# Low parts of the weights on VectorE instead of GpSimd, and a shorter general path

## The chip, the cores and the metric

One Trainium2 chip, one of its cores. The metric is the time on the device for one execution of the program, in microseconds. The kernel before took 546.93 us (median of 3 runs, 546.54 to 547.39).

## What is computed

The reference is a gated linear recurrence over 768 steps for 4 x 8 heads of 48 channels, followed by a feed-forward block over the 3072 tokens that come out of it:

```python
for t in range(S):                                   # B, H, S, D = 4, 8, 768, 48
    state = alpha[:, :, t, :, None] * state + k_t (x) v_t
    y[:, :, t] = q_t @ state
x = y as (B*S, H*D)                                  # 3072 x 384
h = x @ w_in                                         # w_in 384 x 2048
g = h * tanh(softplus(h))
out = g @ w_out                                      # w_out 2048 x 384
```

`q`, `k`, `v` and `alpha` are float32; the weights come as float64, which on the chip are pairs of 32-bit words.

## The kernel before

**Two paths.** `fast_path` computes the result and, beside it, a set of conditions on the inputs (no overflow, no vanishing decay, weights in range). They end in one word, `good` (L886). All five engines load that word (L1018) and branch on it (L1019): if a condition fails, `general_path` computes everything again in a slow and safe way; if all hold, they jump over its code to the end of the program. With the inputs timed here they jump. The general path's instructions stand in each engine's stream between the branch and the place where it lands.

**The fast path.** The 768 steps are cut into 24 chunks of 128 steps (4 batches, 6 chunks each). For each chunk `attention(n)` loads q, k and alpha (`qka`, two buffers) and v, makes running products of alpha with two scans on VectorE (L472, L484), scales k and q (L480, L494), forms the scores on TensorE (L508), masks them (L516), forms y (L531) and updates the state (L499, L658). y is split into a high and a low part in fp32r, the inputs of the feed-forward block.

The feed-forward block runs in 106 units, `unit(c0, nt, f, ...)`: `nt` chunks (2 or 4) times one of 16 slices `f` of the hidden channels. A unit is 9 matmuls up (L695), a chain of ScalarE and VectorE work on the result (L703 to L729) and 3 matmuls down for each chunk (L764). Every factor is held as a high and a low part, so each product takes three matmuls.

**The weights.** `weight(f)` prepares slice f of both weight matrices (m = 0, 1), 32 preparations in all. VectorE builds the float32 word from the two halves of the float64 (L352, L357, L362), ScalarE rounds it to the high part `hi` (L367), and GpSimd subtracts `hi` from the word to give the low part `lo` (L370). `lo` is needed by the matmuls of the units of slice f.

**The order.** All of it is written as tasks with an engine, a cost (time on the engine, time until the result is there), a due key and dependencies. `Plan.order` runs through them as a list scheduler and emits each engine's instructions in the order that it finds: of the tasks that can begin soonest it takes the one with the lowest key. Tasks marked `port=True` share one resource in the plan (VectorE and GpSimd work on SBUF never overlap in it). Where the plan finds TensorE idle for longer than a filler matmul and 0.1 us, between its times 2.4 and 130 us, it emits a filler (L822), a matmul on zeros whose result is overwritten. The plan only sets the order; on the chip every instruction waits for its semaphores.

**The fillers before.** The first 16 are bf16 with 384 columns; the 63 after them take nine forms in groups of seven (bf16 or fp32r, 96 or 128 rows and columns, 128 to 512 columns wide); the rest are again bf16 with 384 columns.

Of the kernel before, what the change touches and what calls it, by code (L numbers as in the profile page):

```python
# [9 lines left out]
F32 = mybir.dt.float32  # L10
F32R = mybir.dt.float32r
BF16 = mybir.dt.bfloat16
I32 = mybir.dt.int32
U32 = mybir.dt.uint32
AF = mybir.ActivationFunctionType
# [13 lines left out]
P = 128  # L29
# [28 lines left out]
CHECK_FROM = 45.0  # L58
CHECK_STEP = 2.0
COLD = 16  # L60
EACH = 7
FORMS = [
    (False, P, P, DM, True), (True, P, P, DM, True), (True, P, 96, DM, True),
    (True, P, P, 512, True), (True, P, P, 256, True), (False, P, 96, DM, True),
    (True, P, P, DM, False), (True, 96, P, DM, True), (True, P, P, 128, True),
]
LAST_FORM = COLD + EACH * len(FORMS)
FILL_BANKS = ("o3", "o2", "o1", "o0", "h")
FILL_FROM, FILL_UNTIL = 2.4, 130.0
FILL_MARGIN = 0.1  # L70
EARLY_BANKS = {}
X_PE = 8
W_PE = 0
W_PE_BANKS = ["o2"]
MOVER = lambda n, s, r: "SP"

# [19 lines left out]
class Plan:  # L96
# [121 lines left out]
COST = {  # L218
    "load part": (0.7, 3.3), "load q": (1.8, 5.0), "load v": (0.7, 4.0), "load w": (2.0, 5.0),
    "move": (0.63, 2.5), "store": (0.47, 3.0),  # L220
    "cold fill": (0.321, 0.36), "off": (0.4, 0.65), "w off": (0.95, 1.2), "lead": (0.27, 0.38), "bits": (0.47, 0.58), "w hi": (0.42, 0.56), "w lo": (0.95, 1.08),
    "w check": (0.92, 1.2),
    "scan": (1.16, 1.27), "inverse": (0.09, 0.21), "mult": (0.6, 0.72), "check": (0.2, 0.34),
    "state": (0.365, 0.4), "state0": (0.31, 0.35), "mask": (0.63, 0.77),
    "scores": (1.1, 1.35), "y0": (1.1, 1.4), "y": (2.0, 2.25), "turn": (0.4, 0.65),
    "turned": (0.43, 0.57), "update": (0.75, 1.05),
    "x3 hi": (0.16, 0.3), "x3 lo": (0.2, 0.32), "x hi": (0.39, 0.53), "x lo": (0.48, 0.59),
    "down": (0.531, 0.8), "stash": (0.4, 0.53), "join": (0.47, 0.59), "result": (0.5, 0.7),
}
for _n in range(1, 5):  # L230
    _c = 128 * _n
    COST["up", _n] = (9 * (0.4333e-3 * _c + 0.009), 9 * (0.4333e-3 * _c + 0.009) + 0.25)
    COST["exp", _n] = (0.22 + 0.836e-3 * _c, 0.32 + 0.836e-3 * _c)
    COST["act", _n] = (0.105 + 0.836e-3 * _c, 0.24 + 0.836e-3 * _c)
    COST["ln", _n] = (0.19 + 0.836e-3 * _c, 0.33 + 0.836e-3 * _c)
    COST["dve", _n] = (0.075 + 1.045e-3 * _c, 0.19 + 1.045e-3 * _c)

for _n in (128, 256, DM, 512):
    for _real in (False, True):
        _c = _n / 2400 + (0.017 if _real else 0.0035)  # L240
        COST["fill", _real, _n] = (_c, _c + 0.03)

EXPLORE = None

# [1 line left out]
def fast_path(ctx, tc, qka, v, w, out, good):  # L246
# [84 lines left out]
    def weight(f):  # L331
# [12 lines left out]
        for m in range(2):  # L344
            hi, lo = (wo[:, z, f : f + 1, :] if m else wi[:, z, :, fs] for z in range(2))
            as_hi = lambda t, hi=hi: t.rearrange("p (s f) -> p s f", f=hi.shape[-1])
            lead = plan.buffer("lead")
            words = lambda z, m=m: stage.tile[:, m, :, z]

            def begin(m=m, lead=lead, words=words):  # L350
                new(lead, [P, DM], f"w_lead{f}_{m}", dtype=I32)
                nc.vector.tensor_scalar(  # L352
                    lead.tile, words(1), 3, 0x3FFFFFF8, ALU.logical_shift_left, ALU.bitwise_and
                )

            def signs(lead=lead, words=words):
                nc.vector.scalar_tensor_tensor(  # L357
                    lead.tile, words(1), -0x40000000, lead.tile, ALU.bitwise_and, ALU.bitwise_or
                )

            def ends(lead=lead, words=words):
                nc.vector.scalar_tensor_tensor(  # L362
                    lead.tile, words(0), 29, lead.tile, ALU.logical_shift_right, ALU.bitwise_or
                )

            def upper(lead=lead, hi=hi, as_hi=as_hi):
                nc.scalar.activation(hi, as_hi(lead.tile.bitcast(F32)), AF.Copy)  # L367

            def lower(lead=lead, hi=hi, lo=lo, as_hi=as_hi):
                nc.gpsimd.tensor_tensor(  # L370
                    lo, as_hi(lead.tile.bitcast(F32)), hi.bitcast(F32), ALU.subtract
                )

            k = key + 0.5 * m
            t = add("DVE", *COST["lead"], k, begin, [got], [stage, lead], port=True)
            t = add("DVE", *COST["bits"], k + 0.01, signs, [t], [stage, lead], port=True)
            t = add("DVE", *COST["bits"], k + 0.02, ends, [t], [stage, lead], port=True)
            a = add("ACT", *COST["w hi"], k + 0.03, upper, [t], [lead])
            if f < W_PE:
                bank = plan.buffer(W_PE_BANKS[(2 * f + m) % len(W_PE_BANKS)])  # L380

                def off(bank=bank, lead=lead, hi=hi, as_hi=as_hi, m=m):
                    p = new(bank, [P, NPAIR * C], f"w{f}_{m}", ps)[:, :DM]
                    nc.tensor.matmul(p, ident, lead.tile.bitcast(F32), start=True, stop=False)
                    nc.tensor.matmul(as_hi(p), minus_ident, hi, start=False, stop=True)

                def left(bank=bank, lo=lo, as_hi=as_hi):
                    nc.scalar.activation(lo, as_hi(bank.tile[:, :DM]), AF.Copy)

                t = add("PE", *COST["w off"], k + 0.04, off, [a], [lead, bank])  # L390
                b = add("ACT", *COST["w hi"], k + 0.05, left, [t], [bank])
            else:
                b = add("POOL", *COST["w lo"], k + 0.04, lower, [a], [lead], port=True)
            ready_w[f, m] = [a, b]
# [412 lines left out]
            add("SP", *COST["store"], k, store, [written], [osb])  # L807

    nothing = const.tile([P, NPAIR * C], BF16, name="nothing")  # L810
    nc.vector.memset(nothing, 0.0)
    none_r = const.tile([P, NPAIR * C], F32R, name="none_r")
    nc.scalar.activation(none_r, nothing, AF.Copy)

    def fill(buffer, i):
        real, rows, cols, n, start = FORMS[max(i - COLD, 0) // EACH] if i < LAST_FORM else FORMS[0]
        of = none_r if real else nothing

        def fill():
            if buffer.tile is None:  # L820
                buffer.make()
            nc.tensor.matmul(  # L822
                buffer.tile[:cols, :n], of[:rows, :cols], of[:rows, :n], start=start, stop=True,
                skip_group_check=True,
            )

        return Task("PE", *COST["cold fill" if i < COLD else ("fill", real, n)], None, fill, False)

    plan.fill = fill

# [58 lines left out]
def general_path(ctx, tc, q, k, v, alpha, w_in, w_out, out):  # L889

    nc = tc.nc
    T = 16
    BH = B * H
    dram = ctx.enter_context(tc.tile_pool(name="dram", bufs=1, space=bass.MemoryType.DRAM))
    x_d = dram.tile([B * S, DM], F32, name="x_d")
# [23 lines left out]
                nc.sync.dma_start(dst[:, ds(t0, T), :], yt[b * H : (b + 1) * H])  # L919

    with tc.tile_pool(name="conv", bufs=1) as sb:
        W = 512
        for m, src in enumerate((w_in, w_out)):
            words = src.rearrange("r c -> (r c)").bitcast(I32).rearrange("(p c) -> p c", p=P)
            with tc.For_i(0, DM * FF // P, W) as c0:
                t = sb.tile([P, W, 2], I32, tag="t", name=f"t{m}")
                nc.sync.dma_start(t.rearrange("p c w -> p (c w)"), words[:, ds(c0 * 2, 2 * W)])
                low, high = t[:, :, 0].bitcast(U32), t[:, :, 1]
                lead = sb.tile([P, W], I32, tag="lead", name=f"lead{m}")
                unit = sb.tile([P, W], I32, tag="unit", name=f"unit{m}")  # L930
                f = sb.tile([P, W], F32, tag="f", name=f"f{m}")
                z = sb.tile([P, W], F32, tag="z", name=f"z{m}")
                nc.vector.tensor_scalar(
                    lead, high, 3, 0x3FFFFFF8, ALU.logical_shift_left, ALU.bitwise_and
                )
                nc.vector.scalar_tensor_tensor(
                    lead, high, -0x40000000, lead, ALU.bitwise_and, ALU.bitwise_or
                )
                nc.vector.tensor_scalar(unit, lead, -0x800000, None, ALU.bitwise_and)
                nc.scalar.activation(f, low, AF.Copy, scale=2.0**-52)  # L940
                nc.vector.tensor_tensor(f, f, unit.bitcast(F32), ALU.mult)
                nc.vector.tensor_tensor(f, f, lead.bitcast(F32), ALU.add)
                nc.scalar.activation(z, high.bitcast(F32), AF.Square)
                nc.vector.tensor_scalar(lead.bitcast(F32), z, W_SMALL, -1.0, ALU.is_lt, ALU.mult)
                nc.vector.scalar_tensor_tensor(
                    f, lead.bitcast(F32), 1.0, f, ALU.add, ALU.mult
                )
                nc.vector.tensor_scalar(z, z, W_LARGE, -1.0, ALU.is_lt, ALU.mult)
                nc.vector.tensor_scalar(z, z, 1.0, 3e38, ALU.add, ALU.mult)
                nc.vector.scalar_tensor_tensor(f, z, 1.0, f, ALU.add, ALU.mult)  # L950
                nc.sync.dma_start(w_d[m][:, ds(c0, W)], f)

    with tc.tile_pool(name="moe", bufs=1) as sb, tc.tile_pool(name="pm", bufs=1, space=PSUM) as ps:
        ident = sb.tile([P, P], F32, name="ident_g")
# [131 lines left out]
```

## Time and profile before

| | us |
|---|---|
| median of 3 runs | 546.93 |
| the profiled execution, its own time | 546.43 |
| its span, from the first to the last instruction | 544.7 |
| TensorE busy | 532.1 (98%) |
| VectorE busy | 400.9 (74%) |
| ScalarE busy | 396.5 (73%) |
| GpSimd busy | 51.6 (9%) |
| DMA, mean rate | 100 GB/s |

PE is TensorE, PEld its weight load, DVE is VectorE, ACT ScalarE, POOL GpSimd, SP the queue that issues the DMAs. A "q" behind an engine's name is its sequencer: instructions that wait, load registers or branch. Busy shares are means over stages with different limits. Fillers count as busy time of TensorE. Instructions of one engine overlap a little: the next starts before the end of the last is recorded.

### The profile page before, as it was taken

How to read it: one execution, taken by the hardware profiler on the slowest of the kernel's cores; microseconds unless marked ns; L12 is line 12 of the kernel's file. 1: busy time of each engine (PE TensorE's matmuls, PEld its weight loads, DVE VectorE, ACT ScalarE, POOL GpSimd, SP SyncE). 2: the span in 40 equal slices, each digit the busy share in tenths (PEclk: the TensorE clock that was granted, in tenths of full speed). 3: DMA queues.
4: the chain of work that ended last, by engine and by line, in shares of the span. 5: the costliest groups of instructions: out<-in, count | busy, mean ns of one | idle time of the engine just before them, and what ended most of it. 6: DMA issues, size and time to landing. Idle time of an engine off the chain costs nothing.

```text
span 544.7 us, 9438 instructions
## 1 busy us (share of the span) xinstructions
PE 532.1 (98%) x3405; PEld 471.8 (87%) x3405; DVE 400.9 (74%) x715; ACT 396.5 (73%) x907; POOL 51.6 (9%) x45
## 2 busy tenths in 40 slices
PE   7999999999999999999999999999999999999994
PEld 4787899988898888888899888899988889998994
DVE  7999999999998699777974567885458744545441
ACT  1565779999688997997867755567775567787773
POOL 2222104514331000000000000000000000000000
PEclk9999999999999999999999999999999999999998
DMA  7665536221453677556220032220042000010001
GB/s 246 191 171 177 163 86 205 63 112 58 143 157 117 193 235 259 176 190 192 71 72 2 29 102 74 74 73 1 5 126 75 9 7 1 14 45 1 1 0 63
DMA packets 21812, 54.20 MB, mean 100 GB/s; under 512 B 4000, under 2 KB 14752, under 8 KB 21760
## 3 DMA queue, kind: packets, MB, share of 16 engines
q1 hardware_dynamic: 21760, 53.55, 32.1%
q8 instruction: 28, 0.46, 0.4%
q14 instruction: 24, 0.20, 0.1%
HBM read 46.45 MB, written 4.72 MB: 94 GB/s over the span
## 4 chain that ended last, share of the span: by engine, by line
PE 81%; DVE 11%; DMA 4%; ACT 1%; issue 1%; SPq 0%; ACTq 0%
PE o L764 35%; PE h L695 33%; PE y L531 6%; PE sc L508 4%; DMA qka<-in_qka_dram 4%; PE u L646 2%; DVE rest L472 2%; PE kb L637 1%; DVE probs L516 1%; DVE qka L484 1%; DVE w_lead L357 1%; DVE w_lead L352 1%; DVE y L713 1%; DVE w_lead L362 1%; DVE t L722 1%
## 5 line engine op out<-in xcount | busy, mean ns | idle before, releaser
L764 PE MATMUL o<-wo,g 128*128 128x384 f32 x1152 | 229.2, 342 | 0.0
L695 PE MATMUL h<-xs,wi 128*128 128x512 f32 (+1 forms) x954 | 218.3, 373 | 0.4 <-DVE y L713 0.4
L764 PEld LDWEIGHTS o<-wo,g 128*128 128x128 f32 x1152 | 202.0, 188 | 9.5 <-issue 0.7
L695 PEld LDWEIGHTS h<-xs,wi 128*128 128x128 f32 x954 | 167.5, 188 | 27.1 <-DVE y L713 0.7
L703 ACT ACTIVATE u<-h 128x512 f32<-128x512 f32 (+1 forms) x106 | 58.8, 554 | 90.7 <-PE h L695 90.5
L713 DVE SCALAR_TENSOR_TENSOR y<-u,h 128x512 f32<-128x512 f32 (+1 forms) x106 | 67.0, 633 | 54.0 <-ACT u L703 53.5
L729 DVE TENSOR_TENSOR g<-t,g 128x512 fp32r<-128x512 f32 (+1 forms) x106 | 68.7, 649 | 50.6 <-ACT g L726 50.3
L716 ACT ACTIVATE t<-t,tenth 128x512 f32<-128x512 f32 (+1 forms) x106 | 71.9, 679 | 2.1
L722 DVE SCALAR_TENSOR_TENSOR t<-y,t 128x512 f32<-128x512 f32 (+1 forms) x106 | 67.4, 636 | 8.1 <-ACT t L719 7.8
L726 ACT ACTIVATE g<-t 128x512 fp32r<-128x512 f32 (+1 forms) x106 | 61.6, 582 | 8.6 <-DVE t L722 6.2
L709 ACT ACTIVATE t<-u 128x512 f32<-128x512 f32 (+1 forms) x106 | 62.7, 591 | 3.2 <-DVE g L729 0.7
L719 ACT ACTIVATE t<-t 128x512 f32<-128x512 f32 (+1 forms) x106 | 61.6, 581 | 0.7
L472 DVE TENSOR_TENSOR_SCAN rest<-qka,behind 112x516 f32<-112x516 f32 x24 | 31.6, 1317 | 8.7 <-DMA qka<-in_qka_dram 8.7
L516 DVE COPY_PREDICATED probs<-causal,sc 128x512 f32<-128x512 uint32 x48 | 32.6, 728 | 1.9 <-PE sc L508 1.8
L508 PEld LDWEIGHTS sc<-qka 48*128 48x128 f32 x384 | 24.1, 187 | 8.2 <-issue 4.2
L484 DVE TENSOR_TENSOR_SCAN qka<-qka,ahead 112x516 f32<-112x516 f32 x24 | 31.0, 1293 | 0.0
L370 POOL TENSOR_TENSOR wo<-w_lead,wo 128x384 fp32r<-128x384 f32 x16 | 26.0, 1623 | 50.7 <-ACT wo L367 50.7
L508 PE MATMUL sc<-qka 48*128 48x128 f32 x384 | 28.8, 285 | 1.7 <-ACT wo L367 1.1
L370 POOL TENSOR_TENSOR wi<-w_lead,wi 128x384 fp32r<-128x384 f32 x16 | 22.2, 1390 | 66.0 <-ACT wi L367 66.0
L531 PE MATMUL y<-probs,v 128*64 128x128 f32 (+1 forms) x384 | 26.6, 278 | 0.3 <-DVE ahead L477 0.2
L531 PEld LDWEIGHTS y<-probs,v 128*64 128x64 f32 (+1 forms) x384 | 20.5, 129 | 4.3 <-DVE probs L516 1.1
L531 PE MATMUL y<-qka,state 112*112 112x128 f32 x160 | 20.9, 273 | 0.0
(78 smaller groups left out, 408.1 us busy)
## 6 DMA issues: line engine op xcount, KB each, us to landing
qka<-in_qka_dram SPq DMA_DIRECT2D x23, 674.2 KB, 5.3
ws<-in_wp_dram SPq DMA_DIRECT2D x16, 768.0 KB, 4.8
wc<-in_wp_dram SPq DMA_DIRECT2D x16, 768.0 KB, 4.9
v<-in_vp_dram SPq DMA_DIRECT2D x24, 192.0 KB, 3.4
out_dram<-osb SPq DMA_DIRECT2D x16, 192.0 KB, 1.9
xs<-x SPq DMA_DIRECT2D x144, 16.0 KB, 2.4
out_dram<-part SPq DMA_DIRECT2D x8, 192.0 KB, 2.4
qka<-in_qka_dram SPq DMA_DIRECT2D x2, 224.0 KB, 3.7
```

The source lines that it names most:

```text
L508: nc.tensor.matmul(p[a][:, j], K()[r : r + D, j], Q()[r : r + D, j], start=True, stop=True)
L531: nc.tensor.matmul(o, l, r, start=m < (2 if first else 1), stop=m >= len(ops) - 2, skip_group_check=True,)
L695: nc.tensor.matmul(p[:, :N], wi[:, z, s, fs], x[:, a, s], start=m == 0, stop=m == len(passes) - 1)
L703: nc.scalar.activation(wide(u), wide(h), AF.Exp, scale=-1.0, accum_out=uchk[:, at : at + 1])
L709: nc.scalar.activation(wide(t), wide(u), AF.Square, bias=1.0, scale=2.0)
L713: nc.vector.scalar_tensor_tensor(wide(y), wide(u), 0.5, wide(h), ALU.add, ALU.mult)
L716: nc.scalar.activation(wide(t), wide(t), AF.Ln, bias=tenth, scale=0.1)
L719: nc.scalar.activation(wide(t), wide(t), AF.Exp, scale=-1.0)
L722: nc.vector.scalar_tensor_tensor(wide(t), wide(y), 0.4, wide(t), ALU.mult, ALU.mult)
L726: nc.scalar.activation(g.tile[:, 0, :N], wide(t), AF.Copy)
L729: late[mybir.EngineType.DVE] = nc.vector.tensor_tensor(g.tile[:, 1, :N], wide(t), g.tile[:, 0, :N].bitcast(F32), ALU.subtract)
L764: made = nc.tensor.matmul(o.tile[:, :DM], g.tile[:, a, j * C : (j + 1) * C], wo[:, z, f], start=begins and m == 0, stop=end and m == 2,)
```

## The change

The low part of every weight slice is computed by VectorE (`f >= W_DVE` holds for all f, with `W_DVE = 0`), with the cost 0.47 us in the plan instead of 0.95 us. The fillers all take one form. `none_r` and the ScalarE instruction that writes it go; `nothing` becomes 384 columns wide. Some costs of the plan are set anew. The general path takes two steps to a turn of its recurrence loop instead of 16, and converts both weight matrices in one loop with tiles half as wide instead of two loops.

```diff
-EACH = 7
-FORMS = [
-    (False, P, P, DM, True), (True, P, P, DM, True), (True, P, 96, DM, True),
...
-LAST_FORM = COLD + EACH * len(FORMS)
...
+W_DVE = 0
...
-    "cold fill": (0.321, 0.36), "off": (0.4, 0.65), "w off": (0.95, 1.2), "lead": (0.27, 0.38), "bits": (0.47, 0.58), "w hi": (0.42, 0.56), "w lo": (0.95, 1.08),
+    "cold fill": (0.321, 0.36), "fill": (0.1635, 0.2), "off": (0.4, 0.58), "w off": (0.95, 1.2), "lead": (0.27, 0.38), "bits": (0.47, 0.58), "w hi": (0.42, 0.56), "w lo": (0.95, 1.08),
...
-    "scores": (1.1, 1.35), "y0": (1.1, 1.4), "y": (2.0, 2.25), "turn": (0.4, 0.65),
-    "turned": (0.43, 0.57), "update": (0.75, 1.05),
+    "scores": (1.12, 1.28), "y0": (1.1, 1.16), "y": (2.0, 2.02), "turn": (0.4, 0.64),
+    "turned": (0.43, 0.57), "update": (0.73, 0.98),
...
-    COST["up", _n] = (9 * (0.4333e-3 * _c + 0.009), 9 * (0.4333e-3 * _c + 0.009) + 0.25)
-    COST["exp", _n] = (0.22 + 0.836e-3 * _c, 0.32 + 0.836e-3 * _c)
+    COST["up", _n] = (9 * (0.4333e-3 * _c + 0.009), 9 * (0.4333e-3 * _c + 0.009) + 0.205)
+    COST["exp", _n] = (0.22 + 0.836e-3 * _c, 0.29 + 0.836e-3 * _c)
...
-            if f < W_PE:
+            if f >= W_DVE:
+                def left_here(lead=lead, hi=hi, lo=lo, as_hi=as_hi):
+                    nc.vector.tensor_tensor(
+                        lo, as_hi(lead.tile.bitcast(F32)), hi.bitcast(F32), ALU.subtract
+                    )
+
+                b = add("DVE", *COST["bits"], k + 0.04, left_here, [a], [lead], port=True)
+            elif f < W_PE:
...
-    nothing = const.tile([P, NPAIR * C], BF16, name="nothing")
+    nothing = const.tile([P, DM], BF16, name="nothing")
     nc.vector.memset(nothing, 0.0)
-    none_r = const.tile([P, NPAIR * C], F32R, name="none_r")
-    nc.scalar.activation(none_r, nothing, AF.Copy)
...
-                buffer.tile[:cols, :n], of[:rows, :cols], of[:rows, :n], start=start, stop=True,
+                buffer.tile[:, :DM], nothing[:, :P], nothing, start=True, stop=True,
...
-        return Task("PE", *COST["cold fill" if i < COLD else ("fill", real, n)], None, fill, False)
+        return Task("PE", *COST["cold fill" if i < COLD else "fill"], None, fill, False)
...
-    T = 16
+    T = 2
...
-        W = 512
-        for m, src in enumerate((w_in, w_out)):
-            words = src.rearrange("r c -> (r c)").bitcast(I32).rearrange("(p c) -> p c", p=P)
-            with tc.For_i(0, DM * FF // P, W) as c0:
...
+        W = 256
+        words = [
+            src.rearrange("r c -> (r c)").bitcast(I32).rearrange("(p c) -> p c", p=P)
+            for src in (w_in, w_out)
+        ]
+        with tc.For_i(0, DM * FF // P, W) as c0:
+            t = sb.tile([P, 2, W, 2], I32, name="words")
+            for m in range(2):
+                nc.sync.dma_start(
...
```

## Rows read from the trace of the kernel before

**Rows 1.** The head of the page, its busy times by engine, and the chain of work that ended last, by engine.

```profile
span 544.7 us, 9438 instructions
PE 532.1 (98%) x3405; PEld 471.8 (87%) x3405; DVE 400.9 (74%) x715; ACT 396.5 (73%) x907; POOL 51.6 (9%) x45
PE 81%; DVE 11%; DMA 4%; ACT 1%; issue 1%; SPq 0%; ACTq 0%
```

**Rows 2.** Busy time by stretch: the stretch and its length, then busy time and instructions of PE, PEld, DVE, ACT, POOL, then the granted TensorE clock, the DMA share and GB/s.

```profile
10.00:28.00 18.00, 17.46 (x151) 13.91 (x149) 16.39 (x29) 7.42 (x20) 3.22 (x4) 1.00 0.69 217
28.00:50.00 22.00, 20.56 (x171) 16.75 (x168) 21.64 (x37) 12.71 (x38) 7.06 (x5) 1.00 0.67 201
50.00:110.00 60.00, 59.72 (x475) 55.81 (x474) 58.00 (x126) 49.47 (x146) 17.07 (x10) 1.00 0.43 126
110.00:170.00 60.00, 59.07 (x324) 52.41 (x322) 58.07 (x100) 49.90 (x106) 20.75 (x14) 1.00 0.34 109
170.00:260.00 90.00, 90.00 (x625) 79.59 (x626) 70.68 (x124) 81.08 (x188) 0.00 (x0) 1.00 0.64 203
```

**Rows 3.** The same view for the fillers alone (line 822): busy time and instructions of PE and PEld.

```profile
10.00:28.00 18.00, 8.75 (x43) 6.16 (x41) 1.00 0.69 217
28.00:50.00 22.00, 8.64 (x47) 5.12 (x47) 1.00 0.67 201
50.00:110.00 60.00, 0.66 (x3) 0.21 (x3) 1.00 0.43 126
```

**Rows 4.** The low parts on GpSimd (line 370): count, shortest, median and longest in ns, first and last start in us.

```profile
L370 POOL TENSOR_TENSOR wi<-w_lead,wi x16: 1012/1166/2446, 17.3 to 163.4; 128x384 fp32r<-128x384 f32 x16
L370 POOL TENSOR_TENSOR wo<-w_lead,wo x16: 1006/1246/3442, 18.3 to 167.9; 128x384 fp32r<-128x384 f32 x16
```

**Rows 5.** VectorE instructions by line. First the groups (count, busy us, mean ns, idle before), then the same lines with shortest, median and longest in ns.

```profile
L472 DVE TENSOR_TENSOR_SCAN rest<-qka,behind 112x516 f32<-112x516 f32 x24 | 31.6, 1317 | 8.7 <-DMA qka<-in_qka_dram 8.7
L484 DVE TENSOR_TENSOR_SCAN qka<-qka,ahead 112x516 f32<-112x516 f32 x24 | 31.0, 1293 | 0.0
L362 DVE SCALAR_TENSOR_TENSOR w_lead<-ws,w_lead 128x384 int32<-128x384 int32 x32 | 18.7, 584 | 0.2
L480 DVE TENSOR_TENSOR qka<-qka,rest 112x512 f32<-112x512 f32 x24 | 16.9, 703 | 0.0
L499 DVE TENSOR_TENSOR state<-state,rest 48x192 f32<-48x192 f32 x40 | 16.8, 419 | 0.4
L352 DVE TENSOR_SCALAR w_lead<-ws 128x384 int32<-128x384 int32 x32 | 13.5, 427 | 0.0
...
L472 DVE TENSOR_TENSOR_SCAN rest<-qka,behind x24: 1212/1232/2047, 4.3 to 419.3; 112x516 f32<-112x516 f32 x24
L484 DVE TENSOR_TENSOR_SCAN qka<-qka,ahead x24: 1217/1226/2052, 6.2 to 423.1; 112x516 f32<-112x516 f32 x24
L362 DVE SCALAR_TENSOR_TENSOR w_lead<-ws,w_lead x32: 526/552/1266, 15.9 to 166.7; 128x384 int32<-128x384 int32 x32
L480 DVE TENSOR_TENSOR qka<-qka,rest x24: 658/665/1485, 5.6 to 424.8; 112x512 f32<-112x512 f32 x24
L499 DVE TENSOR_TENSOR state<-state,rest x40: 323/351/1077, 45.1 to 428.6; 48x192 f32<-48x192 f32 x40
L352 DVE TENSOR_SCALAR w_lead<-ws x32: 335/352/1176, 14.3 to 163.9; 128x384 int32<-128x384 int32 x32
```

**Rows 6.** VectorE in order of time between 28 and 50 us: start, us, instruction, count, and the idle time before it.

```profile
28.29 1.74 DVE L472 TENSOR_TENSOR_SCAN rest<-qka,behind 112x516 f32<-112x516 f32 x1 [0.72 <-DMA qka<-in_qka_dram]
...
34.00 0.55 DVE L357 SCALAR_TENSOR_TENSOR w_lead<-ws,w_lead 128x384 int32<-128x384 int32 x1
34.47 2.05 DVE L472 TENSOR_TENSOR_SCAN rest<-qka,behind 112x516 f32<-112x516 f32 x1
...
42.67 1.49 DVE L480 TENSOR_TENSOR qka<-qka,rest 112x512 f32<-112x512 f32 x1
...
45.15 1.42 DVE L499 TENSOR_TENSOR state<-state,rest 48x192 f32<-48x192 f32 x2
```

**Rows 7.** The end of the program. First line 1019, the branch and what each engine does at the place where it lands (count, shortest, median and longest in ns, first and last start in us); then the SP queue's semaphore waits of the end (line 1081); then who the SP queue waited for after 536 us (us in total, times, longest).

```profile
L1019 DVEq COMPARE_BRANCH  x1: 84/84/84, 539.8 to 539.8; - x1
L1019 ACTq EVENT_SEMAPHORE  x1: 17/17/17, 540.2 to 540.2; - x1
L1019 POOLq EVENT_SEMAPHORE  x1: 17/17/17, 540.2 to 540.2; - x1
L1019 PEldq EVENT_SEMAPHORE  x1: 51/51/51, 540.3 to 540.3; - x1
L1019 DVEq EVENT_SEMAPHORE  x1: 21/21/21, 543.7 to 543.7; - x1
...
L1081 SPq EVENT_SEMAPHORE  x10: 17/28/2287, 541.2 to 544.7; - x10
...
SPq L1081 <- DVEq L1019: 2.3, 1, 2.3
```

**Rows 8.** DMA queues that fetch instructions: packets, MB and share, over the span (q8 and q14), and for 533 to 545 us alone (q14, the last line).

```profile
q8 instruction: 28, 0.46, 0.4%
q14 instruction: 24, 0.20, 0.1%
...
q14 instruction: 5, 0.04, 1.0%
```

More of the change, by code (lines that the diff above doesn't have):

```diff
@@ L60 @@
 COLD = 16
-EACH = 7
-FORMS = [
-    (False, P, P, DM, True), (True, P, P, DM, True), (True, P, 96, DM, True),
-    (True, P, P, 512, True), (True, P, P, 256, True), (False, P, 96, DM, True),
-    (True, P, P, DM, False), (True, 96, P, DM, True), (True, P, P, 128, True),
-]
-LAST_FORM = COLD + EACH * len(FORMS)
 FILL_BANKS = ("o3", "o2", "o1", "o0", "h")
@@ L236 @@
     COST["dve", _n] = (0.075 + 1.045e-3 * _c, 0.19 + 1.045e-3 * _c)
[L238 to L241, printed above, removed]
 EXPLORE = None
@@ L807, in unit @@
             add("SP", *COST["store"], k, store, [written], [osb])
-    nothing = const.tile([P, NPAIR * C], BF16, name="nothing")
+    nothing = const.tile([P, DM], BF16, name="nothing")
     nc.vector.memset(nothing, 0.0)
-    none_r = const.tile([P, NPAIR * C], F32R, name="none_r")
-    nc.scalar.activation(none_r, nothing, AF.Copy)
     def fill(buffer, i):
-        real, rows, cols, n, start = FORMS[max(i - COLD, 0) // EACH] if i < LAST_FORM else FORMS[0]
-        of = none_r if real else nothing
         def fill():
@@ L921, in general_path @@
     with tc.tile_pool(name="conv", bufs=1) as sb:
-        W = 512
-        for m, src in enumerate((w_in, w_out)):
-            words = src.rearrange("r c -> (r c)").bitcast(I32).rearrange("(p c) -> p c", p=P)
-            with tc.For_i(0, DM * FF // P, W) as c0:
[L926 to L934, printed above, removed]
-                )
[L936 to L951, printed above, removed]
@@ new lines, in general_path @@
+        W = 256
[7 more added lines that the diff above has]
+                nc.sync.dma_start(
+                    t[:, m].rearrange("p c w -> p (c w)"), words[m][:, ds(c0 * 2, 2 * W)]
+                )
+            low, high = t[:, :, :, 0].bitcast(U32), t[:, :, :, 1]
+            lead = sb.tile([P, 2, W], I32, name="lead_g")
+            unit = sb.tile([P, 2, W], I32, name="unit_g")
+            f = sb.tile([P, 2, W], F32, name="f_g")
+            z = sb.tile([P, 2, W], F32, name="z_g")
+            nc.vector.tensor_scalar(
+                lead, high, 3, 0x3FFFFFF8, ALU.logical_shift_left, ALU.bitwise_and
+            )
+            nc.vector.scalar_tensor_tensor(
+                lead, high, -0x40000000, lead, ALU.bitwise_and, ALU.bitwise_or
+            )
+            nc.vector.tensor_scalar(unit, lead, -0x800000, None, ALU.bitwise_and)
+            nc.scalar.activation(f, low, AF.Copy, scale=2.0**-52)
+            nc.vector.tensor_tensor(f, f, unit.bitcast(F32), ALU.mult)
+            nc.vector.tensor_tensor(f, f, lead.bitcast(F32), ALU.add)
+            nc.scalar.activation(z, high.bitcast(F32), AF.Square)
+            nc.vector.tensor_scalar(lead.bitcast(F32), z, W_SMALL, -1.0, ALU.is_lt, ALU.mult)
+            nc.vector.scalar_tensor_tensor(f, lead.bitcast(F32), 1.0, f, ALU.add, ALU.mult)
+            nc.vector.tensor_scalar(z, z, W_LARGE, -1.0, ALU.is_lt, ALU.mult)
+            nc.vector.tensor_scalar(z, z, 1.0, 3e38, ALU.add, ALU.mult)
+            nc.vector.scalar_tensor_tensor(f, z, 1.0, f, ALU.add, ALU.mult)
+            for m in range(2):
+                nc.sync.dma_start(w_d[m][:, ds(c0, W)], f[:, m])
```

## Prediction, made before the changed kernel was run

> **What bounds the kernel now.** I read the head of the page and its chain first. The span is 544.7 us, TensorE is busy for 98% of it and makes up 81% of the chain that ended last [rows 1]. A mean hides that fillers count as busy, so I read the busy time by stretch next, for all and then for the fillers alone. Between 28 and 50 us TensorE shows 20.56 us of 22, but 8.64 us of that are fillers, 47 of them, and VectorE stands at 21.64 us [rows 2, 3]: up to 50 us VectorE sets the pace and TensorE pads. From 50 us on there are three more fillers, and TensorE has 59.72 of 60, 59.07 of 60 and then 90.00 of 90 us [rows 2, 3]. VectorE stays at 58.0 of 60 us up to 170 us, then falls to 70.68 of 90 [rows 2]. From 50 us on the time is thus a fixed amount of matrix work in one queue, and a change of VectorE's load moves the end in two ways only: it moves the point, near 50 us, at which TensorE is no longer short of work, or it brings VectorE so far behind, before 170 us, that TensorE runs dry again.
>
> I read the end of the program last. All engines branch at about 539.8 us. ScalarE, GpSimd and TensorE do their next thing at 540.2 to 540.3 us, VectorE at 543.7 us, and nothing in its work holds it there [rows 7]. SP's queue waits for that: one of its ten waits takes 2287 ns where the median takes 28, and the view of waits names VectorE's sequencer for 2.3 us [rows 7]. The last microseconds of the span hang on VectorE's jump.
>
> **The change part by part.** The sum is made against the profiled execution, 546.43 us (its span of 544.7 and 1.73 around it); the median of the runs is 0.5 us above it.
>
> *GpSimd's work goes.* 32 instructions of 1.2 us median [rows 4] leave an engine that is idle otherwise. Nobody is seen to wait for them, so their own time is worth nothing. Their disturbance is: VectorE's instructions that read SBUF show a long tail. Mean less median, times the count: the two scans 24 x 85 ns and 24 x 67 ns, L480 24 x 38, L362 32 x 32, L352 32 x 75, L499 40 x 68, in all 2.0 + 1.6 + 0.9 + 1.0 + 2.4 + 2.7 = 10.6 us [rows 5]. All of these have their longest case some 0.7 to 0.8 us above the median. I take this as what GpSimd costs VectorE; it goes.
>
> *VectorE gets 32 subtractions of 128x384.* No row shows this one on VectorE. The nearest, with the same width and one operand from the same tile, is L362 with a median of 552 ns [rows 5]; in a full queue the next instruction starts after 0.47 us (L357 at 34.00, the scan at 34.47) [rows 6]. From below 0.35 us (L352, one operand), from above 0.67 us (L480, 512 columns) [rows 5]. I take 0.47: 32 x 0.47 = 15.0 us come, 10.6 go, +4.4 us of VectorE's time (by the two ends 32 x 0.35 - 10.6 = 0.6 and 32 x 0.67 - 10.6 = 10.8). Where it falls decides.
>
> Up to 28 us four slices' halves (x4) [rows 2]: 4 x 0.47 = 1.9 us, but VectorE is idle for 1.6 us of that stretch, waiting for loads and scores [rows 2], and these tasks come behind the chunks' own by their keys. On the path: 0.3 us, at most 1.9.
>
> From 28 to 50 us five more [rows 2]: +2.35 us. Gone are four visible stretchings: the scan at 28.29, 1.74 instead of 1.23; the scan at 34.47, 2.05 instead of 1.23; L480 at 42.67, 1.49 instead of 0.67; the pair at 45.15, 1.42 instead of about 0.7 [rows 5, 6]: 0.51 + 0.82 + 0.82 + 0.7 = 2.85 us. Net -0.5. Two of the four lie on scans, the first link of a chunk's chain.
>
> After 50 us the other 23 cost 10.8 us against 10.6 - 2.85 = 7.8 regained: +3.0 us on an engine with 58.0 + 58.1 of 120 us taken up to 170 us [rows 2]. What hides them is the 3.9 us that are left there and TensorE's backlog: units queue behind each other, so a low part that comes later by its place in VectorE's queue is still early. If that cover were gone, 3.0 us would be lost, no more. Behind each subtraction in VectorE's queue stand scans and the units' own steps (L713, L722, L729); the subtraction waits for ScalarE's L367, so a late ScalarE now also holds VectorE up. I price that at nothing, because the plan places it only when it holds ScalarE to be done, and keep 23 waits of 0.05 us in the range.
>
> Early part in all: +0.3 - 0.5, which I take as 0.
>
> *Fillers, `none_r`, new costs.* The fillers stand where TensorE has nothing else to do (8.64 us of 22 between 28 and 50 us) [rows 3], so another form of them is worth nothing; the cover is VectorE's pace. `none_r` is one ScalarE instruction before the first work. The lower latencies (0.02 to 0.24 us) make the plan place a task a little sooner. After 50 us a task that was placed too soon stalls its queue; TensorE's idle time there is 0.28 + 0.93 us up to 170 us [rows 2], so some tenths are the price, and as much can be gained before 50 us. Zero, with 1 us to either side.
>
> *The general path gets shorter.* It doesn't run, but it is jumped over. Why does VectorE alone take 3.9 us from 539.8 to 543.7? Five packets of q14 fall into the last 12 us, of 24 in the whole span [rows 8], so instructions were fetched there. [...] Counted in the program of the kernel before, VectorE has 225 instructions between the branch and the landing, more than anyone: ScalarE 108, GpSimd 91, SP 161. The first two land in 0.4 us. [...] The change takes out 14 x 5 = 70 instructions of the recurrence and one conversion loop of VectorE, 9 instructions with 25 for the loop itself: 225 - 70 - 34 = 121. [...] VectorE then lands at 540.2 as the others do and SP's 2287 ns shrink to the 28 of their neighbours: -2.26 us. The bounds are 0 and -2.26: the wait of 2287 ns that ends with VectorE at 543.7 began at about 541.5, so SP's own chain is late next and nothing more can come. I take -2.26, since 121 is nearest to ScalarE's 108, which land at once [rows 7].
>
> [...]
>
> Sum: 546.43 + 0 - 2.26 = 544.2 us for a profiled execution, 544.7 us for the median.
>
> **The rivals.**
>
> *The early part gains as well (14%).* All 2.85 us between 28 and 50 us are regained on the path and the subtractions fall into waits. For it speaks that the stretched scans are the first links of their chunks; against it, that VectorE waits only 22.0 - 21.64 = 0.4 us there [rows 2]. 546.93 - 2.26 - 2.85 = 541.8 us. [...]
>
> *The jump stays slow (13%).* The 3.9 us are not the distance of the jump. For it speaks that a hint for this branch is already given and TensorE's landing, with 152 instructions, is quick; against it the packets. Then only the early 0 is left: 546.9 us.
>
> *VectorE's queue becomes the bound (13%).* All nine early subtractions stand in the chain of a chunk, and what GpSimd's leaving gives back falls on work that nothing waits for: 9 x 0.47 = 4.2 us later at 50 us. 546.93 - 2.26 + 4.2 = 548.9 us. It decides from 3.4 us on (seven of the nine), where the gain at the end is used up and 0.2% passed. For it speaks VectorE's 21.64 of 22 us; against it the 2.85 us read above.
>
> **How the numbers follow.** My forecast has 60%: 544.7 us, with its own range from 543.7 (early -1) to 546.0 (early +1.3). 0.2% is 1.1 us and about what a measurement of this kernel can tell from no change: faster is under 545.8, slower over 548.0. Faster: 57 of the 60 and the first rival's 14, 71%. Slower: 12 of the third's 13 and 1 of the second's, 13%. The same: the other 16%. The range from 542.4 to 547.4 takes in the forecast, the slow jump with 0.5 to its upper side and half of the first rival; it leaves out the third and the other half of the first, 20%.
>
> **What would show each step.** GpSimd's busy time falls to about 3.4 us. VectorE shows 32 subtractions of 0.55 us, the means of L472, L484, L499 and L352 come down to their medians, and its busy time rises by 4 us or less. TensorE's fillers end within 1.3 us of 50 us. VectorE's sequencer lands at line 1019 within 0.5 us of its branch and no SP wait of line 1081 is over 0.5 us. [...]

## The result and the profile after

The changed kernel takes 538.31 us (median of 4 runs, 537.35 to 538.78) where the kernel before took 546.73 beside it: 0.984 of its time, 95% interval 0.983 to 0.986, or 8.4 us less. The forecast was 544.7, with a range from 542.4 to 547.4. The span of the profiled execution fell from 544.7 to 535.6 us.

The page of the changed kernel: span, busy times by engine, and the chain that ended last.

```profile
span 535.6 us, 9408 instructions
PE 527.7 (99%) x3395; PEld 467.3 (87%) x3395; DVE 400.7 (75%) x747; ACT 394.7 (74%) x906; POOL 3.5 (1%) x13
...
PE 96%; DMA 1%; DVE 1%; ACT 1%; SPq 0%; issue 0%
```

TensorE makes up 96% of the chain where it was 81%, and VectorE 1% where it was 11 [rows 1]. VectorE has 32 instructions more and the same busy time.

The changed kernel's busy time by stretch (columns as in [rows 2]), then its fillers alone (columns as in [rows 3]). Lines of the attention and of the units stand four lower in its file than in the kernel before: L691 is L695 there.

```profile
10.00:28.00 18.00, 17.50 (x154) 11.91 (x153) 17.51 (x33) 7.66 (x21) 0.00 (x0) 1.00 0.67 212
28.00:50.00 22.00, 21.92 (x190) 17.45 (x189) 21.94 (x44) 14.61 (x46) 0.00 (x0) 1.00 0.66 199
50.00:110.00 60.00, 59.84 (x461) 56.40 (x459) 59.65 (x141) 50.60 (x149) 0.00 (x0) 1.00 0.42 134
110.00:170.00 60.00, 60.00 (x337) 53.83 (x337) 58.67 (x113) 51.04 (x110) 0.00 (x0) 1.00 0.36 120
...
28.00:50.00 22.00, 7.04 (x36) 3.19 (x36) 1.00 0.66 199
```

Between 28 and 50 us TensorE now does 21.92 - 7.04 = 14.9 us of real work; it was 20.56 - 8.64 = 11.9 [rows 2, 3]. Its idle time from 50 to 170 us is 0.16 us; it was 0.28 + 0.93 [rows 2].

The end of the changed kernel: the branch (line 1014 here) and SP's waits (line 1076).

```profile
L1014 DVEq COMPARE_BRANCH  x1: 84/84/84, 532.9 to 532.9; - x1
L1014 DVEq EVENT_SEMAPHORE  x1: 21/21/21, 533.5 to 533.5; - x1
...
L1076 SPq EVENT_SEMAPHORE  x10: 17/28/28, 534.3 to 535.6; - x10
```

VectorE lands 0.6 us after its branch, not 3.9, and SP's longest wait is 28 ns, not 2287 [rows 7]. From branch to end the program takes 535.6 - 532.9 = 2.7 us; it was 544.7 - 539.8 = 4.9. So 2.2 us of the 9.1 by which the profiled span fell lie behind the branch, where the forecast had them, and 6.9 ahead of it, where the forecast had none.

### The profile page after: what moved, and what is told of

The parts are those of the page before. It is cut to its first block, busy times and chain, and to the rows that moved or that the text cites. A ratio compares the mean times of both kernels' runs of the same rounds, so it can differ in the third digit from the quotient of the medians.

```text
span 535.6 us, 9408 instructions
## 1 busy us (share of the span) xinstructions
PE 527.7 (99%) x3395; PEld 467.3 (87%) x3395; DVE 400.7 (75%) x747; ACT 394.7 (74%) x906; POOL 3.5 (1%) x13
## 4 chain that ended last, share of the span: by engine, by line
PE 96%; DMA 1%; DVE 1%; ACT 1%; SPq 0%; issue 0%
PE o L760 39%; PE h L691 38%; PE y L527 8%; PE sc L504 5%; PE u L642 3%; PE o L813 2%; PE kb L633 2%; DMA qka<-in_qka_dram 1%; PE y L559 0%; ACT osb L794 0%; SPq L446 0%; DVE rest L468 0%; DVE probs L512 0%; SPq L450 0%; ACT xs L545 0%
## 5 line engine op out<-in xcount | busy, mean ns | idle before, releaser
L691 PE MATMUL h<-xs,wi 128*128 128x512 f32 (+1 forms) x954 | 217.8, 373 | 0.0
L691 PEld LDWEIGHTS h<-xs,wi 128*128 128x128 f32 x954 | 167.4, 188 | 26.8 <-DVE y L709 0.3
L725 DVE TENSOR_TENSOR g<-t,g 128x512 fp32r<-128x512 f32 (+1 forms) x106 | 67.2, 636 | 47.8 <-ACT g L722 47.2
L722 ACT ACTIVATE g<-t 128x512 fp32r<-128x512 f32 (+1 forms) x106 | 61.5, 583 | 7.5 <-DVE t L718 4.5
L468 DVE TENSOR_TENSOR_SCAN rest<-qka,behind 112x516 f32<-112x516 f32 x24 | 29.5, 1229 | 10.2 <-DMA qka<-in_qka_dram 10.1
L480 DVE TENSOR_TENSOR_SCAN qka<-qka,ahead 112x516 f32<-112x516 f32 x24 | 29.4, 1224 | 0.0
L813 PE MATMUL o<-nothing 128*128 128x384 bf16 x103 | 21.8, 356 | 2.4 <-DVE behind L270 2.4
L699 ACT ACTIVATION_READ_ACCUMULATOR u<-h 128x1 f32 x106 | 20.6, 194 | 0.0
```

Of the source, the lines that this page charges most:

```text
L691: nc.tensor.matmul(p[:, :N], wi[:, z, s, fs], x[:, a, s], start=m == 0, stop=m == len(passes) - 1)
L699: nc.scalar.activation(wide(u), wide(h), AF.Exp, scale=-1.0, accum_out=uchk[:, at : at + 1])
L722: nc.scalar.activation(g.tile[:, 0, :N], wide(t), AF.Copy)
L725: late[mybir.EngineType.DVE] = nc.vector.tensor_tensor(g.tile[:, 1, :N], wide(t), g.tile[:, 0, :N].bitcast(F32), ALU.subtract)
```

## Experiments

All differences below are from the kernel before timed on the same chip (545.9 to 546.9 us); intervals are of the ratio to it.

**One part alone, in twos.** The low parts alone:

```diff
+W_DVE = 0
-            if f < W_PE:
+            if f >= W_DVE:
...
+                b = add("DVE", *COST["bits"], k + 0.04, left_here, [a], [lead], port=True)
```

> The kernel before with the low parts on VectorE, in the plan and on the chip, and nothing else of the change. Theory A (GpSimd's disturbance of VectorE was worth more than I priced): nearly all of the 6.9 us that the changed kernel gains ahead of the branch come from here, 540 to 541.5 us; the slow landing at line 1019 stays at 3.9 us. Theory B (the new costs of the plan gain): no more than 1.5 us, 545.5 us or over. Theory C (what I forecast for this part): 546.7 us with 1 us to either side.

Measured: 541.96 us, 0.9925 (0.990 to 0.995), -4.1 us. That is four times the bound of theory C and the larger part of the 6.9 us, but not "nearly all" of them, as theory A had it. The slow landing stays, 4.3 us in this execution.

The general path alone (T = 2, one conversion loop):

> The kernel before with the shorter general path alone. The distance of VectorE's jump is the cause of the slow landing: 544.4 us, 2.26 us under the kernel before, and VectorE's sequencer lands within 0.5 us of its branch. Rival (the landing is slow for another reason and came right by the shift of 32 instructions): no change, 546.7 us.

Measured: 543.07 us, 0.9939 (0.992 to 0.996), -3.0 us. VectorE's branch and landing:

```profile
L1023 DVEq COMPARE_BRANCH  x1: 84/84/84, 538.5 to 538.5; - x1
L1023 DVEq EVENT_SEMAPHORE  x1: 21/21/21, 539.2 to 539.2; - x1
```

0.7 us instead of 3.9, with the fast path untouched: the shorter general path is the cause. A shift of VectorE's queue by 32 instructions is not: with the shift and the long path (e1_lows_only, and e4_before_on_vector below) the landing takes 4.3 and 3.9 us, without the shift and with the short path (e3_after_on_gpsimd) 0.6. The branch itself came at 538.5 in this execution and at 539.8 in that of [rows 7], with the same instructions ahead of it: single executions differ by about 1 us.

**Order against engine.** The changed kernel with `nc.gpsimd.tensor_tensor` in place of `nc.vector.tensor_tensor` in `left_here`, and the kernel before with the opposite swap in `lower`; neither plan is touched:

> The changed kernel, its plan untouched (the subtractions are planned as VectorE's, at 0.47 us), but each of them is issued to GpSimd at the same place of the order. Theory A (disturbance): VectorE's scans are stretched again, and of the 6.9 us at least 4 are lost: 542 us or over. Theory D (the order found by the new plan gains, whoever computes): at most 1.5 us are lost, 538 to 540 us.

> The kernel before, its plan untouched (the subtractions are planned as GpSimd's, at 0.95 us), but each of them is issued to VectorE at the same place of the order. Theory A (disturbance): 542 us or under, most of the gain ahead of the branch, with the slow landing left. Theory D (order): 546 us or over, since VectorE gets 15 us more work in the old order.

Measured: 541.94 us (0.9925, 0.990 to 0.995), -4.1, for the first; 543.69 us (0.9957, 0.995 to 0.997), -2.3, for the second. With the 2.25 us of the end taken off where the general path is short, this gives a table of the work ahead of the branch:

| us against before | issued to GpSimd | issued to VectorE |
|---|---|---|
| plan of before | 0 | -2.3 |
| changed plan | -1.8 | -6.2 (-5.5 on another chip) |

Both theories hold in part. Getting off GpSimd is worth 2.3 us in the old order and about 4 in the new; the plan (order, costs and fillers together) is worth 1.8 on GpSimd and 3 to 4 on VectorE.

Where on the way is this gained? A mark that every kernel has is the first unit with four chunks (its matmuls up are 512 columns wide). It starts, in the kernel before, in the same order on VectorE (e4_before_on_vector), in the new order on GpSimd (e3_after_on_gpsimd), and in the changed kernel, at:

```profile
104.11 2.25 PE L695 MATMUL h<-xs,wi 128*128 128x512 f32 x9
103.42 2.25 PE L695 MATMUL h<-xs,wi 128*128 128x512 f32 x9
101.90 2.25 PE L691 MATMUL h<-xs,wi 128*128 128x512 f32 x9
98.80 2.25 PE L691 MATMUL h<-xs,wi 128*128 128x512 f32 x9
```

From there to VectorE's branch the four take 435.7, 433.7, 435.9 and 434.1 us. So about 2 us are gained after the mark, in either order, when GpSimd's work goes. Ahead of the mark getting off GpSimd gives 0.7 us in the old order, within the 1 us by which executions differ (the same order starts this unit at 103.0 us in e2_general_only and at 104.0 in g1_long_jump_before), and 3.1 us in the new one. VectorE's instructions in the changed kernel:

```profile
L468 DVE TENSOR_TENSOR_SCAN rest<-qka,behind 112x516 f32<-112x516 f32 x24 | 29.5, 1229 | 10.2 <-DMA qka<-in_qka_dram 10.1
L480 DVE TENSOR_TENSOR_SCAN qka<-qka,ahead 112x516 f32<-112x516 f32 x24 | 29.4, 1224 | 0.0
L495 DVE TENSOR_TENSOR state<-state,rest 48x192 f32<-48x192 f32 x40 | 13.9, 347 | 0.4
L341 DVE TENSOR_SCALAR w_lead<-ws 128x384 int32<-128x384 int32 x32 | 10.7, 352 | 0.1
L370 DVE TENSOR_TENSOR wi<-w_lead,wi 128x384 fp32r<-128x384 f32 x16 | 8.8, 549 | 0.0
```

The means are down to the medians of [rows 5]: 1317 to 1229, 1293 to 1224, 419 to 347, 427 to 352. The old order shows whose doing it was: in e4_before_on_vector L472's longest is 1245 ns, where it was 2047. And where TensorE waited in the run with the changed order on GpSimd (third slice's unit, in order of time):

```profile
35.90 1.10 PE L691 MATMUL h<-xs,wi 128*128 128x256 f32 x7 [0.38 <-POOL wi L370]
```

So the statement that nobody waits for GpSimd held for the old order alone. What the new order does shows where the fourth slice is prepared. Its low part on GpSimd and its first unit in the kernel before; then low part, chunk 4's first scan and that unit in the changed kernel:

```profile
41.19 2.42 POOL L370 TENSOR_TENSOR wi<-w_lead,wi 128x384 fp32r<-128x384 f32 x1 [1.05 <-ACT wi L367]
48.66 1.36 PE L695 MATMUL h<-xs,wi 128*128 128x256 f32 x9
```

```profile
38.72 0.55 DVE L370 TENSOR_TENSOR wi<-w_lead,wi 128x384 fp32r<-128x384 f32 x1
39.66 1.23 DVE L468 TENSOR_TENSOR_SCAN rest<-qka,behind 112x516 f32<-112x516 f32 x1
41.25 1.33 PE L691 MATMUL h<-xs,wi 128*128 128x256 f32 x9
```

The slice is ready at 39.3 instead of 43.6 us and its unit runs 7.4 us sooner; chunk 4's scan, which stood at 34.47 [rows 6], comes 5.2 us later. TensorE, short of work there, gets units sooner and chunks later. Most of the 7.4 us is the order alone: with the same order on GpSimd (e3_after_on_gpsimd) the unit stands 5.4 us ahead of the kernel before's already.

```profile
43.26 1.33 PE L691 MATMUL h<-xs,wi 128*128 128x256 f32 x9 [0.22 <-DVE y L709]
```

**The price in the plan.** The low parts on VectorE with GpSimd's old price (the edit is shown against e1_lows_only), and on GpSimd with VectorE's (against the kernel before):

```diff
-b = add("DVE", *COST["bits"], k + 0.04, left_here, [a], [lead], port=True)
+b = add("DVE", *COST["w lo"], k + 0.04, left_here, [a], [lead], port=True)
```

> The kernel before with the low parts on VectorE in the plan and on the chip, but with the price of 0.95 us that GpSimd's had. It differs from e1_lows_only (4.1 us faster than before) in this price alone. Theory D (the plan orders better because it no longer charges twice what a low part takes): most of the order's share is lost, 543.5 us or over, as in e4_before_on_vector. Rival (it is the engine in the plan, not the price: VectorE's queue is free to choose): as e1_lows_only, 542 us.

Measured: 553.72 us, 1.0108 (1.007 to 1.014), +6.9 us. Neither side expected that: 11 us between this and e1_lows_only, from one price in the plan; but for the fillers that the plan adds, the instructions are the same. Where TensorE waited from 50 to 260 us (L703 and L721 here are L695 and L713 of the kernel before):

```profile
PEld h L703 <- DVE y L721: 5.0, 3, 3.0
PE h L703 <- DVE y L721: 4.1, 2, 2.6
```

The matmuls up, which write a unit's `h`, and their weight loads wait for the VectorE step L721 (`times`), which reads `h`, for 4.1 and 5.0 us in all; so an earlier unit's step holds a later unit up.

```diff
-    ... "w lo": (0.95, 1.08),
+    ... "w lo": (0.47, 0.58),
```

> The kernel before, low parts on GpSimd in the plan and on the chip, with the price of 0.47 us in the plan instead of 0.95. If the price alone makes the better order: 1.5 to 2 us faster than before, 544.5 us, as the changed plan on GpSimd is when the end is left out. If the order gains only where the low parts stand in VectorE's queue: no change within 1 us.

Measured: 549.47 us, 1.0065 (1.004 to 1.009), +2.6 us. The price alone doesn't do it; too low a price hurts as well. Here TensorE waits for units' last step (from 50 to 260 us):

```profile
PEld o L764 <- DVE g L729: 4.7, 6, 1.3
PE o L764 <- DVE g L729: 2.7, 5, 0.9
```

Both are slower than the two kernels whose price lies near what the chip takes on that engine (e1_lows_only with 0.47, where a subtraction on VectorE takes 0.47 in a full queue of the changed kernel, from 33.47 us to the next start at 33.94; the kernel before with 0.95 for GpSimd's 1.0 to 1.2 [rows 4]). Four kernels do not make this a rule.

**The new costs and the fillers.** The new costs in the kernel before, and the old costs in the changed kernel:

> The kernel before with the new costs of the plan alone (off, scores, y0, y, turn, update, up, exp); low parts on GpSimd, fillers and general path as before. If the new costs gain by themselves: about the 2 us by which the changed kernel is ahead of e1_lows_only at its branch, 544 us. If they gain only where VectorE computes the low parts: no change, within 1 us.

> The changed kernel with the eight old costs in the plan, its fillers, low parts and general path as changed. If the new costs are what sets the changed kernel ahead of e1_lows_only and e2_general_only together: 2 us slower than the changed kernel, about 539.5 us where that is 537.5. If the fillers of one form or the lost ScalarE instruction do it: as the changed kernel, within 0.7 us.

Measured: 545.05 us (0.9967, 0.995 to 0.998), -1.8, and 539.14 us (0.9868, 0.984 to 0.990), -7.7. The second was too wide to tell from the changed kernel, so it was timed again beside it, with the two large parts together (low parts and general path, nothing else):

> The changed kernel, for comparison on this chip: 8.5 us under the kernel before.

> The changed kernel with the old costs. If the new costs are worth something beside the rest: 1 to 1.5 us over the changed kernel. If not: within 0.5 us of it.

> The kernel before with the low parts on VectorE and the shorter general path, its old costs and fillers of nine forms. If the two parts are all of the gain: within 0.5 us of the changed kernel. If the fillers and none_r count: as far over the changed kernel with old costs as they are worth, up to 1 us; 4.1 and 2.3 us under the kernel before, 6.4 in all.

Measured on one chip, in this order: 538.20 us (0.9856, 0.984 to 0.987), 539.71 us (0.9882, 0.987 to 0.990) and 540.03 us (0.9887, 0.987 to 0.991). The new costs are worth about 1.5 us, the fillers and `none_r` nothing that can be told. Low parts and general path make 5.9 of the 7.8 us; 4.1 of e1_lows_only and 2.2 behind the branch would be 6.3.

Fewer fillers (`FILL_MARGIN` 0.5 for 0.1 in the changed kernel):

> The changed kernel with fillers only where the plan sees TensorE idle for a filler and 0.5 us instead of 0.1. The chain of the changed kernel runs through TensorE and its fillers from 12 us on. If fillers hold up real work there: 0.5 to 2 us faster than the changed kernel (537.5), near 536.5 us. If they stand where it would wait anyway: the same within 0.7 us. [...]

Measured: 538.14 us, 0.985 (0.983 to 0.988): the same as the changed kernel within the noise (it was not timed beside it on this chip), and the first unit with four chunks starts at 98.8 us in both. The fillers that were left out stood where TensorE would wait anyway, although the chain runs through fillers.

**The length of the jump.** One conversion loop but T = 16, in the kernel before, where VectorE then jumps over 192 instructions by a count in the program, and in the changed one, where it jumps over 191. These lengths lie between the 121 of the changed kernel and the 225 of the kernel before:

> The kernel before with one conversion loop but 16 steps to a turn: VectorE jumps over 192 instructions. [...]

> [...]

VectorE's landing in the first, then in the second:

```profile
L1023 DVEq COMPARE_BRANCH  x1: 84/84/84, 540.1 to 540.1; - x1
L1023 DVEq EVENT_SEMAPHORE  x1: 21/21/21, 544.1 to 544.1; - x1
```

```profile
L1014 DVEq COMPARE_BRANCH  x1: 84/84/84, 534.3 to 534.3; - x1
L1014 DVEq EVENT_SEMAPHORE  x1: 21/21/21, 538.4 to 538.4; - x1
```

Slow both times, 4.0 and 4.1 us (one execution each, 546.86 and 541.10 us). In these runs VectorE's jumps over 191 instructions and more take 3.9 to 4.3 us to land and those over 121 and 122 take 0.6 to 0.7; SP's over 161 took 0.5 us in the kernel before, from 540.1 to 540.6. What decides between them is not shown. One run speaks against length alone. In e12_price_047_gpsimd, whose general path is that of the kernel before, TensorE's branch over the same 152 instructions took 3.4 us to land instead of the 0.45 to 0.54 of the five other profiled executions with that path:

```profile
L1019 PEldq COMPARE_BRANCH  x1: 3367/3367/3367, 542.5 to 542.5; - x1
L1019 PEldq EVENT_SEMAPHORE  x1: 51/51/51, 546.0 to 546.0; - x1
```

The cause is not shown. It is a single execution, and it cost nothing, since VectorE landed later still.

**A version that beats both.** The changed kernel with `W_DVE = 4` and `W_PE = 4`: the low parts of the first four slices go to TensorE and ScalarE.

> The changed kernel, but the low parts of the first four slices are computed by TensorE and ScalarE (the subtraction in PSUM by a matmul with a minus identity, then a copy out), which the kernel has code for. Up to 50 us VectorE is full and TensorE has fillers. If VectorE's time still sets the pace there: 8 x 0.47 = 3.8 us at most are gained, 1 to 3 us likely, 535 to 536.5 us. If the changed kernel is bound by loads, buffers and TensorE's own queue by then: within 1 us of it, 537.5 us, or slower, because two matmuls and a copy come in.

> The changed kernel with the low parts of the first four slices on TensorE and ScalarE. If VectorE still bounds the first 50 us: 0.7 us or more under the changed kernel; else within 0.5 us of it.

Measured: 537.45 us (0.9839, 0.981 to 0.987), from which nothing can be told, then 536.68 us (0.9825, 0.981 to 0.984) beside the changed kernel's 538.20: 1.5 us faster. Its fillers from 28 to 50 us in the second run:

```profile
28.00:50.00 22.00, 0.82 (x3) 0.23 (x3) 1.00 0.69 205
```

7.04 us of fillers have become 0.82: TensorE does VectorE's work there, and the first 50 us still had something to give.

## Why the prediction was wrong, point by point

- *The general path*: right in place and size. -2.26 us forecast, 2.2 by the profile; the second rival (the jump stays slow) is out. VectorE lands in 0.6 us with 121 instructions, as I took it from ScalarE's 108; but what makes a landing slow is shown by no run: VectorE's jumps over 191, 192 and 225 instructions took 3.9 to 4.3 us and those over 121 and 122 took 0.6 to 0.7, and TensorE's over 152 took 3.4 us in e12_price_047_gpsimd where it took 0.45 to 0.54 in five other executions.
- *VectorE's load*: right for what comes, too small for what goes. I forecast 32 x 0.47 us to come; the subtractions last 0.55 and take 0.47 each in a full queue (one starts at 33.47 us, the next instruction at 33.94). I let 10.6 us go; by the means of [rows 5] and above the same six lines gave back 2.1 + 1.7 + 1.1 + 0.9 + 2.9 + 2.4 = 11.1 (L362 and L480 by 34 and 39 ns each, now at 550 and 664). But lines that I had not counted gave back 3.6 more (L357 1.2, the units' steps L713, L722 and L729 2.4), so the balance of 4 us that I forecast came out at about nothing: 400.9 us before, 401.4 in e4_before_on_vector, 400.7 in the changed kernel. And the nine low parts that I placed before 50 us are eight: one that runs from 27.93 to 28.94 us is counted in both stretches of [rows 2]. That makes the early sum 0.5 us better, not 5.
- *"Early part in all: +0.3 - 0.5, which I take as 0"*: this step failed, in what it was computed from. It weighs VectorE's work before and after in the same order. In the same order it is about right: the first unit with four chunks starts at 103.4 us in e4_before_on_vector, and between 103.0 and 104.1 us in three profiled executions of the old fast path. But the change also alters the plan, and the new order brought the fourth slice's unit forward (5.4 us by itself, 7.4 together with the change of engine); the first unit with four chunks starts at 98.8 us in the changed kernel, 4 to 5 us sooner.
- *"What hides them is ... TensorE's backlog"*: this failed too, by about 2 us. I let what VectorE regains after 50 us be worth nothing, because TensorE had work in its queue. In the same order the way from the first unit with four chunks to the branch is 2 us shorter without GpSimd (433.7 us against 435.7). About half of it are the 0.28 + 0.93 us of TensorE's idle time from 50 to 170 us that I listed as small. They are gone when GpSimd leaves, in the old order (0.08 + 0.00 in e4_before_on_vector) as in the new (0.16 + 0.00 in the changed kernel):

```profile
50.00:110.00 60.00, 59.92 (x477) 56.17 (x476) 59.23 (x137) 49.84 (x148) 0.00 (x0) 1.00 0.46 140
110.00:170.00 60.00, 60.00 (x330) 53.89 (x329) 58.48 (x116) 51.00 (x108) 0.00 (x0) 1.00 0.35 115
```

  The other half does not show as idle time; what it consists of stays open.
- *"Fillers, `none_r`, new costs: zero, with 1 us to either side"*: right for the fillers, mis-sized for the costs: 1.5 us in the new order, 1.8 in the old.
- *The first rival* (14%, 541.8 us) had the right sign and the wrong mechanism: it put all of its gain before 50 us, by the stretched scans alone; the same order without GpSimd gained 2.3 us, most of them after 104 us, and disturbance and order together made 6.2.
- *The signs*: GpSimd's 3.5 us, subtractions of 0.55 us, the means down to the medians and SP's waits came as written; VectorE's landing took 0.6 us where I allowed 0.5. VectorE's busy time stayed at 400.7 us, within the 4 more that were allowed. One sign failed: the fillers were to end within 1.3 us of 50 us, and the last ends at 46.8. It is the sign of the step that failed, the early part.

In sum: 2.2 us at the end, which were forecast. Ahead of the branch, where nothing was: 4.1 us from the low parts, of which 2.3 come in the old order and 1.8 by the new one, and 1.5 from the costs; the rest, 0 to 0.6 us, is within the noise. Why the greedy plan finds a better order at 0.47 us on VectorE is seen in where slice 4 went, but not shown for each step of it.

## What to carry to other kernels

Where a planner sets the order, a changed cost is a changed program: price the new order, not the moved work alone, and widen the range by what one number in the plan can do (here 11 us from 0.47 to 0.95). The interference cost more in the better order (about 4 us) than in the old one (2.3), so it is worth taking out first and tuning the order after it. A queue that is full on average still runs dry at moments: 1.2 us of 120 that looked small were part of the gain. Look behind the last result too: code that is never run, but jumped over, took 2.2 us.

## What the runs showed of the hardware

- VectorE's jumps over 191, 192 and 225 instructions that don't run (g2_long_jump_after, g1_long_jump_before, and e1_lows_only, e4_before_on_vector and the kernel before) took 3.9 to 4.3 us to land; those over 121 (changed kernel, e3_after_on_gpsimd) and 122 (e2_general_only) took 0.6 to 0.7 us. TensorE's jump over 152 took 0.45 to 0.54 us in five profiled executions but 3.4 us in e12_price_047_gpsimd; the cause is not shown.
- The GpSimd subtractions of 128x384 took 1.0 us at least, 1.2 by the median [rows 4]; on VectorE the median is 0.55 us in the changed kernel. Beside them some of VectorE's instructions ran up to 0.8 us longer: L480 at 42.67 us took 1.49 us [rows 6] during the one from 41.19 to 43.61 us, against a median of 0.67 [rows 5]. Without them its longest is 0.69 us (L476 of the changed kernel), and L472's 1.25 us (e4_before_on_vector) instead of 2.05. In all VectorE got back about what the move costs it (400.9 us busy before, 400.7 after).
- With 36, 23 or 3 fillers between 28 and 50 us (changed kernel, e9_fewer_fillers, h4_early_on_pe_again) the granted clock of TensorE was 1.00 in that stretch.
